# A written order of all engines extended from step 21 to step 95, with a DMA turn from unit 14 on: windowed attention and two expert layers on one core

## The chip, the core and the metric

The kernel runs on one core of a Trainium2 chip. A core has five engines that each run their own instructions in order and meet only through semaphores: TensorE (PE in the profile, with its weight loads as PEld) for matmuls, VectorE (DVE), ScalarE (ACT), GpSimd (POOL) and SyncE (SP), which here issues nearly all DMAs. Matmuls read SBUF and write PSUM; ACT and DVE read PSUM, so everything that PE makes passes through one of them. The metric is the device time of one execution in microseconds (us), lower is better; the profile of one execution tells where it went.

## The reference, cut to what matters

```python
# attention: 4 batches, 8 heads, 576 positions, 64 wide; each row sees itself and the 63 before it
scores = q @ k.T / 8;  scores = where(0 <= i - j < 64, scores, -1e9)
attn = exp(scores - max);  attn = attn / (sum(attn) + 1e-9);  x = attn @ v      # x: 2304 x 512
# first layer, 512 -> 2048 -> 512
h = x @ w_in;  g = h if h >= 1 else 0 if h <= -1 else (h + 1)**2 / 4;  x2 = g @ w_out
# second layer: each row goes to the one of 8 experts with the largest x2 @ w_gate
out[row] = gate_w[row] * (relu(x2[row] @ w1[e]) @ w2[e])
```

All inputs are float32 and the result is float32.

## The kernel before

**Precision.** A float32 factor is kept as two fp32r tiles, hi and lo, and a product is made of three passes (hi·hi, lo weight·hi, hi·lo). So x, the weights and g exist twice, and the lo part is a subtraction on DVE (or POOL).

**Blocks and steps.** The 2304 rows are cut into seven blocks of 256, 384, 256, 256, 384, 384 and 384 rows. A *step* of the first layer handles one of 16 slices of 128 hidden columns for one block: `layer1` (L413, 12 matmuls of 256 or 384 columns into PSUM tile `h`), the gate function on ACT and DVE (L424, L425, L428, L434, L436: `a`, then `ghi` and `glo`), and `layer2` (L455, 6 or 9 matmuls of 512 columns into `acc`). The list `SEG` orders the 112 steps: steps 0 to 5 are block 0's first six slices, 6 to 21 block 1, 22 to 31 the rest of block 0, then 16 steps each for blocks 2 (from step 32), 3 (48), 4 (64), 5 (80) and 6 (96). The second layer has 48 steps of the same shape for the most frequent expert, and a tail for the rows of the others.

**Units.** The x of a block comes from attention *units*: unit 2c + hf is four heads of 128 rows. A unit is `u_qk` (mask and score products L275 and L281, small matmuls, into the one PSUM tile `S`), row maximum (L293, DVE; L304, ACT), exponentials (L314, ACT), reciprocal and normalization (L323, L324 and L327), a turn of the 128x512 attention tile, `av` (L370, small matmuls with v) and the hi and lo parts of x (L382 on ACT, L384 on DVE). All units of a block must be done before the block's first step reads them.

**The turn.** Below `DT0` = 24 the turn is four TensorE transposes into PSUM (L351, tile `pt`) and a copy on ACT (L354, `pb`). From unit 24 on DVE first parts the float32 tile into two planes of 16 bits (`halves`, L172, tile `pp`), SP issues a DMA transpose (L334, `pt<-pp`), and ACT joins the planes (`halves`, L170, `pb`).

**The order.** `HEAD` is a written list of short names (`qk0`, `mx0`, `exp0`, `tr0`, `av0` and so on for units, `ab`, `s`, `hc`, `wl` for splitting a weight tile, `ga`, `rl`, `st`, `gh`, `gl`, `gb` for the parts of a step). It covers units 0 to 9, all 32 weight tiles and steps 0 to 21; `in_order` chains its instructions on PE, DVE, ACT and POOL. From step 22 on a loop writes the steps, `PLAN`, `STAGES` and `STAGES3` say in which half step each part of a unit is written, and the framework's scheduler places the instructions on the engines by its own estimates. Loads of q and k (two buffers) and v (one buffer) are written behind `u_qk` and `u_av` by `run_slot`. `BEHIND` ties the mask products of unit 10 to their written place.

**Other places that the change touches.** Units 5, 7, 9, 10, 11 and 13 are normalized on POOL (`NORM_P`, `NORM_V`), all others on DVE. `evac1` takes a finished block from `acc` to `r` (in the new code `take` does: the first tile on ACT, the second on DVE) and writes it twice to DRAM: whole (`x2s`) and as planes (`x2p`). Tiles 0 and 11 of that are parted on DVE, others on ACT (`PS_V`). The x of every block lies in one of two buffers of the pool `xp` (tag `xT`).

Of the kernel before, what the change touches and what calls it, by code (L numbers as in the profile page):

```python
# [19 lines left out]
P = 128  # L20
# [8 lines left out]
NG = TB * P  # L29
# [7 lines left out]
PLAN = {2: (46, 58), 3: (56, 84), 4: (86, 116), 5: (124, 150), 6: (154, 178)}  # L37
# [4 lines left out]
PS_V = (0, 11, 12, 14, 16)  # L42
PJ_V = (6, 16, 32)
PL_V = ()
DT0 = 24
ST3 = (-1, 0, 1, 2, 6, 7)
US_A = (0, 3, 4, 5, 7, 11, 21)
UJ_V = ()
# [8 lines left out]
BEHIND = 10  # L57
# [21 lines left out]
).split()  # L79
NORM_V = (0, 1, 2, 3, 4, 6, 8, 12, 14, 32)  # L80
NORM_P = 14
# [40 lines left out]
def kernel(  # L122
# [132 lines left out]
    def u_qk(u):  # L255
# [12 lines left out]
        for pr in range(2):  # L268
# [4 lines left out]
            for a, r, rows, o in outs:  # L273
                m = 1 + a if kind == 1 + r else 0
                mm = nc.tensor.matmul(  # L275
                    o, ib[rows, 64 * a:64 * a + 64], mb[rows, m], start=True, stop=False
                )
                if u == BEHIND:
                    tc.keep_in_program_order(mm)
# [27 lines left out]
    u_mask = whole(mask_parts)  # L307

# [11 lines left out]
    def norm_parts(u):  # L320
        s = U[u]
        rc = att.tile([P, 4], F32, tag="rc", name="rc", bufs=2)
        nc.vector.tensor_scalar(out=rc, in0=s["sm"], scalar1=1e-9, scalar2=None, op0=ALU.add)  # L323
        nc.vector.reciprocal(rc, rc)  # L324
        yield
        eng = nc.gpsimd if u < NORM_P and u not in NORM_V else nc.vector
        eng.tensor_tensor(  # L327
            out=s["sr"], in0=s["sr"], in1=rc.unsqueeze(2).to_broadcast([P, 4, P]), op=ALU.mult
        )
        if u >= DT0:  # L330
            pl = att.tile([P, 2, 512], U16, tag="t", name="pp", bufs=2)
# [5 lines left out]
            s["tt"] = tt  # L337

    u_norm = whole(norm_parts)

    def tr_parts(u):
        s = U[u]
        if u >= DT0:
            pb = att.tile([P, 4, P], F32, tag="pb", name="pb")
            halves(nc.vector if u in UJ_V else nc.scalar, s["tt"], pb.rearrange("p h q -> p (h q)"), False)
# [10 lines left out]

    u_tr = whole(tr_parts)

    def av_parts(u):
# [17 lines left out]
        if b not in xT:  # L377
            xT[b] = xp.tile([P, 2, KD, NG], F32R, tag="xT", name="xT")
# [6 lines left out]

    u_av = whole(av_parts)
# [14 lines left out]

    STAGES = [(0, u_qk), (0, u_mask), (1, u_exp), (2, u_norm), (3, u_tr), (4, u_av)]
    STAGES3 = list(zip(ST3, (u_qk, u_mask, u_exp, u_norm, u_tr, u_av)))

# [60 lines left out]
    def evac1(b, acc, partial):  # L465
        t0, n = blocks[b]
        nt = n // P
        for p0 in range(0, nt, 2):
            m = min(2, nt - p0)
            r = part.pop((b, p0), None)  # L470
            add = r is not None
            if r is None:
                r = sp.tile([P, 2, 512], F32, tag="st", name="xrow") if not partial else sp.tile([P, 2, 512], F32, tag="st", name="prow")
            for t in range(m):
                if add:
                    nc.vector.tensor_tensor(out=r[:, t], in0=acc[p0 + t], in1=r[:, t], op=ALU.add)
                elif t == 0:
                    nc.scalar.activation(r[:, t], acc[p0 + t], ACTF.Copy)
                else:
                    nc.vector.tensor_copy(r[:, t], acc[p0 + t])  # L480
            if partial:
                part[b, p0] = r
                continue
            for t in range(m):

                o = t0 + (p0 + t) * P
                xr = x2p[o:o + P].rearrange("p (i h q) -> p i h q", i=2, h=2)
                rr = r[:, t].rearrange("p (i q) -> p i q", i=2)
                if "p2" in Z:
                    for i in range(2):  # L490
                        pl = Z["p2"].tile([P, 2, 256], U16, tag="tt", name="pl", bufs=3)
                        halves(nc.vector if o // P in PS_V else nc.scalar, pl, rr[:, i], True)
                        nc.sync.dma_start(xr[:, i], pl)
                    continue
                pl = att.tile([P, 2, 2, 256], U16, tag="t", name="pl", bufs=2)
                eng = nc.vector if o // P in PS_V else nc.scalar
                xv = rr.bitcast(U16).rearrange("p i (q h) -> p i h q", h=2)
                eng.tensor_copy(pl, xv) if eng is nc.vector else eng.activation(pl, xv, ACTF.Copy)
                nc.sync.dma_start(xr, pl)
            if True:  # L500
# [3 lines left out]
                )  # L504

# [330 lines left out]
    ub_ = {}  # L836
    for u, (b, _, _) in enumerate(units):
        ub_.setdefault(b, []).append(u)
# [13 lines left out]
    def plan(us, s0, s1):  # L852
# [240 lines left out]
```

## Time and profile before

| | |
|---|---|
| median of 3 runs (range) | 734.39 us (734.27 to 735.67) |
| the profiled execution | 735.58 us, span of its instructions 733.8 us |
| busy share of the span: PE, DVE, ACT, POOL | 96%, 60%, 55%, 12% |
| granted TensorE clock, mean | 0.982 |
| DMA | 76.85 MB, mean 105 GB/s |

The page also cuts the span into 40 slices with a busy digit for each engine. PE's digits are 5, 7, 9, 7 in the first four slices and 9 in every later one, so what idles on PE idles in the first 73 us. One caution belongs to the page: matmuls are pipelined and their modelled ends overlap the next start, so a busy PE need not be PE at its peak. A timeline therefore has to be read by starts: from the start of one group of matmuls to the start of the next.

### The profile page before, as it was taken

The page shows a single profiled execution, that of the slowest core. Times are in us where ns is not written, and L with a number is a line of the kernel's source. Part 1 is how long each engine was busy: PE and PEld are TensorE (multiplying, and loading weights), DVE is VectorE, ACT ScalarE, POOL GpSimd, SP SyncE. Part 2 cuts the span into 40 slices and gives each one's busy share as a digit, 9 for nine tenths or more (in the row PEclk, how much of TensorE's full clock was granted, in tenths as well). Part 3 has the DMA queues.
Part 4 walks back from the last instruction along what each step waited for, and adds up shares of the span by engine and source line. Part 5 has one row for each costly group of instructions (what it writes and reads, how often), then busy time and mean ns, then how long its engine had stood idle before and what let it go on. Part 6 is the DMA issues. An engine that isn't in the chain of part 4 may idle for free. (4 is left out here: it accounts for less than half of the span.)

```text
span 733.8 us, 12894 instructions
## 1 busy us (share of the span) xinstructions
PE 705.4 (96%) x4843; PEld 614.0 (84%) x4843; DVE 438.2 (60%) x1028; ACT 405.8 (55%) x1004; POOL 88.5 (12%) x86
## 2 busy tenths in 40 slices
PE   5797999999999999999999999999999999999996
PEld 3676998888888888888888898988888989888985
DVE  6898999345344434552554326988799989551110
ACT  6786776577556656774667445566432515163212
POOL 0021000010000000000000000465130202075000
PEclk9697999999999999999999999999999999999999
DMA  9983102324112312531343403353433324043101
GB/s 334 402 344 116 58 1 59 102 87 155 48 33 71 117 48 51 152 94 44 79 152 69 162 1 122 101 141 90 127 82 94 77 82 102 29 151 115 44 0 55
DMA packets 66691, 76.85 MB, mean 105 GB/s; under 512 B 35671, under 2 KB 41559, under 8 KB 66498
## 3 DMA queue, kind: packets, MB, share of 16 engines
q1 hardware_dynamic: 66466, 75.58, 33.1%
q8 instruction: 38, 0.62, 0.4%
q0 software_dynamic: 160, 0.43, 0.2%
q14 instruction: 27, 0.22, 0.1%
HBM read 53.80 MB, written 14.42 MB: 93 GB/s over the span
## 5 line engine op out<-in xcount | busy, mean ns | idle before, releaser
L413 PE MATMUL h<-xT,wi 128*128 128x384 f32 (+1 forms) x1344 | 231.2, 320 | 2.3 <-DVE a L428 1.9
L413 PEld LDWEIGHTS h<-xT,wi 128*128 128x128 f32 x1344 | 213.5, 192 | 15.2 <-DVE a L428 4.2
L455 PE MATMUL acc<-wo,ghi 128*128 128x512 f32 x576 | 154.9, 397 | 0.0
L455 PEld LDWEIGHTS acc<-wo,ghi 128*128 128x128 f32 x576 | 103.7, 188 | 17.6 <-issue 1.5
L550 DVE CUSTOM_DVE_ANT_0 junk<-xg,wgb 128x512 bf16<-128x512 f32 x144 | 114.2, 793 | 3.2
L413 PE MATMUL h<-xT,we 128*128 128x384 f32 x576 | 110.3, 337 | 1.5 <-DVE glo L445 1.5
L413 PEld LDWEIGHTS h<-xT,we 128*128 128x128 f32 x576 | 102.2, 188 | 6.4 <-DVE glo L445 2.2
L428 DVE SCALAR_TENSOR_TENSOR a<-h,a 128x384 f32<-128x384 f32 (+1 forms) x112 | 55.8, 498 | 83.3 <-ACT a L425 82.9
L424 ACT ACTIVATE a<-h,half 128x384 f32<-128x384 f32 (+1 forms) x112 | 59.6, 534 | 60.8 <-PE h L413 58.8
L455 PE MATMUL acc<-wo,glo 128*128 128x512 f32 x288 | 85.3, 394 | 0.0
L436 DVE TENSOR_TENSOR glo<-a,ghi 128x384 fp32r<-128x384 f32 (+1 forms) x106 | 57.9, 547 | 38.3 <-ACT ghi L434 38.1
L455 PE MATMUL acc<-we,ghi 128*128 128x512 f32 x288 | 78.4, 394 | 0.0
L434 ACT ACTIVATE ghi<-a 128x384 fp32r<-128x384 f32 (+1 forms) x112 | 53.1, 476 | 40.6 <-DVE a L428 38.3
L444 ACT ACTIVATE ghi<-h 128x384 fp32r<-128x384 f32 x48 | 23.1, 482 | 75.9 <-PE h L413 65.2
L455 PEld LDWEIGHTS acc<-wo,glo 128*128 128x128 f32 x288 | 53.7, 188 | 12.1 <-issue 0.2
L624 POOL TENSOR_TENSOR we<-er,we 128x512 fp32r<-128x512 f32 x16 | 23.5, 1472 | 312.9 <-PE h L413 300.7
L455 PEld LDWEIGHTS acc<-we,ghi 128*128 128x128 f32 x288 | 53.1, 188 | 8.1
L445 DVE SCALAR_TENSOR_TENSOR glo<-h,ghi 128x384 fp32r<-128x384 f32 x48 | 26.7, 555 | 53.1 <-ACT ghi L444 53.1
L425 ACT ACTIVATE a<-a 128x384 f32<-128x384 f32 (+1 forms) x112 | 53.5, 479 | 3.0
L314 ACT ACTIVATE sr<-S,nm 128x128 f32<-128x128 f32 x136 | 48.2, 367 | 1.2
L455 PE MATMUL acc<-we,glo 128*128 128x512 f32 x144 | 44.1, 395 | 0.0
L891 POOL TENSOR_TENSOR xT<-xj,xT 128x256 fp32r<-128x256 f32 x36 | 31.2, 875 | 88.3 <-ACT xT L890 88.3
(148 smaller groups left out, 690.1 us busy)
## 6 DMA issues: line engine op xcount, KB each, us to landing
qk<-in_qq_dram SPq DMA_DIRECT2D x26, 320.0 KB, 3.1
er<-in_w_dram SPq DMA_DIRECT2D x32, 256.0 KB, 2.8
wraw<-in_wi_dram SPq DMA_DIRECT2D x14, 512.0 KB, 8.0
wraw<-in_wo_dram SPq DMA_DIRECT2D x14, 512.0 KB, 8.0
vt<-in_vv_dram SPq DMA_DIRECT2D x26, 256.0 KB, 2.7
xg<-x2s SPq DMA_DIRECT2D x18, 256.0 KB, 2.8
out_dram<-y SPq DMA_DIRECT2D x18, 256.0 KB, 2.4
qqr<-in_qq_dram SPq DMA_DIRECT2D x10, 320.0 KB, 7.0
```

Of the source, the lines that this page charges most:

```text
L314: nc.scalar.activation(sr[:, h], s["S"][h % 2][:, h // 2 * P:h // 2 * P + P], ACTF.Exp, scale=0.125, bias=s["nm"][:, h:h + 1], accum_out=s ...
L413: nc.tensor.matmul(h[:, :n], w[:, wa, k * P:k * P + P], x[:, xa, k, :n], start=(i == 0), stop=(i == 3 * KD - 1),)
L424: nc.scalar.activation(a[:, :n], h[:, :n], ACTF.Relu, scale=0.5, bias=half[:, 0:1])
L425: nc.scalar.activation(a[:, :n], a[:, :n], ACTF.Square)
L428: nc.vector.scalar_tensor_tensor(out=a[:, :n], in0=h[:, :n], scalar=1.0, in1=a[:, :n], op0=ALU.max, op1=ALU.min)
L434: nc.scalar.activation(hi[:, :n], a[:, :n], ACTF.Copy)
L436: (nc.gpsimd if pool else nc.vector).tensor_tensor(out=lo[:, :n], in0=a[:, :n], in1=hi[:, :n].bitcast(F32), op=ALU.subtract)
L445: nc.vector.scalar_tensor_tensor(out=lo[:, :n], in0=h[:, :n], scalar=0.0, in1=hi[:, :n].bitcast(F32), op0=ALU.max, op1=ALU.subtract,)
L455: nc.tensor.matmul(a, ga[:, t * P:t * P + P], w[:, wa], start=(first and j == 0), stop=(last and j == 2),)
L550: tc.keep_in_program_order(nc.vector.tensor_tensor_reduce(out=junk, in0=xg[t], in1=Z["wgb"][:, e], scale=1.0, scalar=0.0, op0=ALU.mult, op ...
L624: nc.gpsimd.tensor_tensor(out=w[:, 1], in0=raw, in1=w[:, 0].bitcast(F32), op=ALU.subtract)
L891: (nc.vector if 2 * t + i in PL_V else nc.gpsimd).tensor_tensor(out=lo, in0=r, in1=hi.bitcast(F32), op=ALU.subtract)
```

## The change

`HEAD` is extended from step 21 to step 95 and takes in units 10 to 35, with the loads of q, k (`qq`) and v as names of their own and the evacuation of a block in named parts (`ev`, `evd`, `pl`, `ps`). `PLAN`, the stage lists and `BEHIND` go. `DT0` becomes 14, so units 14 to 23 turn by DMA as units 24 to 35 did, and the parting of the planes, the DMA and the joining are three names (`pp`, `tr`, `pb`). Every normalization is on DVE. Block 2's x gets a buffer of its own, `xq`, in the tag that held the last raw weight tiles. Inside `HEAD` all planes of the evacuation are parted on ACT. Steps 96 on are written by the loop as before.

```diff
-PLAN = {2: (46, 58), 3: (56, 84), 4: (86, 116), 5: (124, 150), 6: (154, 178)}
-DT0 = 24
-ST3 = (-1, 0, 1, 2, 6, 7)
-US_A = (0, 3, 4, 5, 7, 11, 21)
+DT0 = 14
-BEHIND = 10
 HEAD = (
...
+    "gl21 qk10 qq12 ga22 mx10 nm10 exp10 gb20 rl22 rc10 nrm10 st22 qk11 gh22 qq13 ga23 mx11 gl22 "
+    "nm11 exp11 tr10 gb21 pb10 rc11 rl23 nrm11 av10 st23 ev0_21 v11 qk12 gh23 evd0_21 hi10 qq14 "
...
 ).split()
-NORM_V = (0, 1, 2, 3, 4, 6, 8, 12, 14, 32)
-NORM_P = 14
...
-        eng = nc.gpsimd if u < NORM_P and u not in NORM_V else nc.vector
-        eng.tensor_tensor(
+        nc.vector.tensor_tensor(
             out=s["sr"], in0=s["sr"], in1=rc.unsqueeze(2).to_broadcast([P, 4, P]), op=ALU.mult
         )
...
+    def tr_parts(u):
+        s = U[u]
         if u >= DT0:
             pl = att.tile([P, 2, 512], U16, tag="t", name="pp", bufs=2)
-            halves(nc.scalar if u in US_A else nc.vector, pl, s["sr"].rearrange("p h k -> p (h k)"), True)
             tt = att.tile([P, 2, 512], U16, tag="t", name="pt", bufs=2)
+            halves(nc.vector, pl, s.pop("sr").rearrange("p h k -> p (h k)"), True)
+            yield
             nc.sync.dma_start(
                 tt.rearrange("p h (c q) -> p (h c) q", q=P), pl.rearrange("p h q -> p (h q)"), transpose=True
             )
+            yield
             pb = att.tile([P, 4, P], F32, tag="pb", name="pb")
-            halves(nc.vector if u in UJ_V else nc.scalar, s["tt"], pb.rearrange("p h q -> p (h q)"), False)
+            halves(nc.scalar, tt, pb.rearrange("p h q -> p (h q)"), False)
...
-            xT[b] = xp.tile([P, 2, KD, NG], F32R, tag="xT", name="xT")
+            xT[b] = (
+                att.tile([P, 2, KD, 256], F32R, tag="qs", name="xq", bufs=QB)
+                if b == 2
+                else xp.tile([P, 2, KD, NG], F32R, tag="xT", name="xT")
+            )
...
+    def pair_parts(b, p0, acc):
+        t0, n = blocks[b]
+        m = len(acc)
+        r = part.pop((b, p0), None)
+        if r is not None:
+            for t in range(m):
+                nc.vector.tensor_tensor(out=r[:, t], in0=acc[t], in1=r[:, t], op=ALU.add)
+        else:
+            r = sp.tile([P, 2, 512], F32, tag="st", name="xrow")
+            take(r, 0, acc[0])
+            if m == 2:
+                yield
+                take(r, 1, acc[1])
+        yield r
+        for t in range(m):
+            pl = att.tile([P, 2, 2, 256], U16, tag="t", name="pl", bufs=2)
+            nc.scalar.activation(pl, xv, ACTF.Copy)
+            yield
+            nc.sync.dma_start(xr, pl)
...
+        if name in ("qq", "v"):
+            (u_load if name == "qq" else v_load)(k)
+            continue
```

What stands on the engines is shown at three places, before first and then now, without the leading numbers.

PE, around unit 17's score product, before: steps 36 and 37. `S<-qk` are its score matmuls, `h` and `acc` the matmuls of the two layers, `av` unit 15's value product, `pt<-ct,sr` unit 16's turn by TensorE.

```order
L281 MATMUL S<-qk 64x128 x3
L413 MATMUL h<-xT,wi 128x256 x8
L370 MATMUL av<-pb,vt 64x64 x8
L413 MATMUL h<-xT,wi 128x256 x4
L455 MATMUL acc<-wo,ghi 128x512 x4
L455 MATMUL acc<-wo,glo 128x512 x2
L413 MATMUL h<-xT,wi 128x256 x12
L455 MATMUL acc<-wo,ghi 128x512 x3
L351 MATMUL pt<-ct,sr 128x128 x4
```

PE, around unit 16's score product and unit 15's value product, now: up to step 39.

```order
L320 MATMUL S<-qk 64x128 x4
L489 MATMUL acc<-wo,ghi 128x512 x4
L489 MATMUL acc<-wo,glo 128x512 x2
L404 MATMUL av<-pb,vt 64x64 x8
L447 MATMUL h<-xq,wi 128x256 x12
```

Before, three of a product's score matmuls stand apart from the other five (which follow three steps later), a value product stands inside a `layer1`, and a turn inside a `layer2`; now each product stands whole, between whole groups of the layers, and this unit's turn is no longer on PE.

ACT, around the joining or copying of unit 14's turned tile `pb`, before. `a` and `ghi` belong to steps, `nm`, `sr` and `xT` to units, `pl` to the evacuation of block 0.

```order
L382 ACTIVATE xT<-av 128x2x128
L304 ACTIVATE nm<-mx 128x4
L314 ACTIVATE sr,sm<-S,nm 128x128 x4
L498 ACTIVATE pl<-prow 128x1024
L354 ACTIVATE pb<-pt 128x512
L424 ACTIVATE a<-h,half 128x256 x2
```

ACT, around unit 14's `pb`, now.

```order
L468 ACTIVATE ghi<-a 128x256 x2
L458 ACTIVATE a<-h,half 128x256
L459 ACTIVATE a<-a 128x256
L211 ACTIVATE pb<-pt 128x2x512
L468 ACTIVATE ghi<-a 128x256
```

The copy out of PSUM has become a joining of planes that waits for a DMA, and a step's `ghi` stands behind it.

DVE, units 7 to 9 in the first 60 us, before. `rc` is unit 7's reciprocal, `mx` unit 8's maximum, `a` and `t` belong to a step and a weight tile.

```order
L323 TENSOR_SCALAR rc<-sm 128x4
L324 RECIPROCAL rc<-rc 128x4
L428 SCALAR_TENSOR_TENSOR a<-h,a 128x256
L293 TENSOR_REDUCE mx<-S 128x2x2
L203 TENSOR_SCALAR t<-t 128x512
```

The same place now.

```order
L360 TENSOR_SCALAR rc<-sm 128x4
L361 RECIPROCAL rc<-rc 128x4
L462 SCALAR_TENSOR_TENSOR a<-h,a 128x256
L363 TENSOR_TENSOR sr<-sr,rc 128x512
L332 TENSOR_REDUCE mx<-S 128x2x2
```

Unit 7's normalization `sr<-sr,rc`, which was on POOL, stands ahead of unit 8's maximum; units 5 and 9 get theirs in the same way.

## Rows read from the trace of the kernel before

**Rows 1.** Busy time by stage (stretch, its length, engines, granted clock, DMA):

```profile
0.00:121.50 121.50, 102.69 (x828) 87.43 (x829) 107.34 (x206) 88.88 (x231) 8.46 (x13) 0.90 0.54 198
121.50:437.00 315.50, 315.32 (x2573) 271.06 (x2572) 141.10 (x321) 194.48 (x535) 3.13 (x3) 1.00 0.29 85
```

**Rows 2.** What PE waited for, 0 to 80 and 80 to 460 us:

```profile
PE pt L351 <- DVE xT L384: 5.9, 4, 2.7
...
PE h L413 <- DVE a L428: 0.2, 1, 0.2
```

**Rows 3.** Timeline of PE, a turn alone: start, length, matmuls, count

```profile
152.54 1.09 PE L455 MATMUL acc<-wo,ghi 128*128 128x512 f32 x4
153.46 0.60 PE L351 MATMUL pt<-ct,sr 128*128 128x128 f32 x4
153.82 0.71 PE L455 MATMUL acc<-wo,glo 128*128 128x512 f32 x2
154.37 1.60 PE L413 MATMUL h<-xT,wi 128*128 128x256 f32 x12
155.80 0.86 PE L455 MATMUL acc<-wo,ghi 128*128 128x512 f32 x3
```

**Rows 4.** Timeline of PE, a whole score product:

```profile
285.57 0.62 PE L455 MATMUL acc<-wo,glo 128*128 128x512 f32 x2
...
286.80 1.48 PE L413 MATMUL h<-xT,wi 128*128 128x384 f32 x7
```

**Rows 5.** Timeline of PE, unit 17's score product in two pieces:

```profile
185.29 0.62 PE L455 MATMUL acc<-wo,glo 128*128 128x512 f32 x2
...
186.24 1.22 PE L413 MATMUL h<-xT,wi 128*128 128x256 f32 x8
...
197.31 1.12 PE L413 MATMUL h<-xT,wi 128*128 128x256 f32 x8
198.36 0.32 PE L281 MATMUL S<-qk 64*64 64x128 f32 x1
...
199.00 1.20 PE L455 MATMUL acc<-wo,ghi 128*128 128x512 f32 x4
```

**Rows 6.** Timeline of PE, a score product cut by a turn:

```profile
217.25 1.36 PE L413 MATMUL h<-xT,wi 128*128 128x256 f32 x10
...
218.93 0.66 PE L351 MATMUL pt<-ct,sr 128*128 128x128 f32 x4
...
220.16 1.20 PE L455 MATMUL acc<-wo,ghi 128*128 128x512 f32 x4
```

**Rows 7.** The parts of a turn on ACT and DVE: count, ns min/median/max, first to last

```profile
L354 ACT ACTIVATE pb<-pt x24: 576/597/667, 10.5 to 267.2; 128x512 f32<-128x512 f32 x24
L170 ACT ACTIVATE pb<-pt x12: 1351/1370/1394, 288.3 to 404.5; 128x1024 uint16<-128x1024 uint16 x12
L172 DVE COPY pp<-sr x12: 682/685/696, 284.4 to 400.7; 128x1024 uint16<-128x1024 uint16 x12
```

**Rows 8.** The DMA turn's line L334: issues, who waited, landing

```profile
L334 SPq DMA_TRANSPOSE pt<-pp x12: 1232/1233/1338, 285.1 to 401.4; - x12
  ACT pb L170: 8.6, 7
DMA to landing us min/median/max: 3.0/3.1/4.8
```

**Rows 9.** Timeline of POOL and DVE in the first 60 us:

```profile
28.60 0.69 DVE L206 SCALAR_TENSOR_TENSOR t<-wraw,t 128x512 int32<-128x512 int32 x1
30.49 1.03 POOL L327 TENSOR_TENSOR sr<-sr,rc 128x512 f32<-128x512 f32 x1 [30.03 <-DVE rc L324]
30.66 1.42 DVE L206 SCALAR_TENSOR_TENSOR t<-wraw,t 128x512 int32<-128x512 int32 x1
41.86 0.68 DVE L327 TENSOR_TENSOR sr<-sr,rc 128x512 f32<-128x512 f32 x1
58.51 0.64 DVE L203 TENSOR_SCALAR t<-t 128x512 int32<-128x512 int32 x1 [0.92 <-ACT t L201]
```

More of the change, by code (lines that the diff above doesn't have):

```diff
@@ L274, in u_qk @@
                 m = 1 + a if kind == 1 + r else 0
-                mm = nc.tensor.matmul(
+                nc.tensor.matmul(
                     o, ib[rows, 64 * a:64 * a + 64], mb[rows, m], start=True, stop=False
                 )
-                if u == BEHIND:
-                    tc.keep_in_program_order(mm)
             for a, r, rows, o in outs:
@@ L336, in norm_parts @@
             )
[L337 to L343, printed above, removed]
+            del pl
+            yield
             pb = att.tile([P, 4, P], F32, tag="pb", name="pb")
-            halves(nc.vector if u in UJ_V else nc.scalar, s["tt"], pb.rearrange("p h q -> p (h q)"), False)
+            halves(nc.scalar, tt, pb.rearrange("p h q -> p (h q)"), False)
             s["pb"] = pb
@@ L355, in tr_parts @@
         s["pb"] = pb
-    u_tr = whole(tr_parts)
     def av_parts(u):
@@ L463, with take @@
     part = {}
-    def evac1(b, acc, partial):
-        t0, n = blocks[b]
[L467 to L473, printed above, removed]
-            for t in range(m):
[L475 to L483, printed above, removed]
+    def take(r, t, a):
+        if t == 0:
+            nc.scalar.activation(r[:, t], a, ACTF.Copy)
+        else:
+            nc.vector.tensor_copy(r[:, t], a)
@@ L484, in evac1 @@
+    def evac1(b, acc):
+        t0, n = blocks[b]
+        for p0 in range(0, n // P, 2):
+            m = min(2, n // P - p0)
+            r = sp.tile([P, 2, 512], F32, tag="st", name="xrow")
+            for t in range(m):
+                take(r, t, acc[p0 + t])
             for t in range(m):
@@ L488, in evac1 @@
                 rr = r[:, t].rearrange("p (i q) -> p i q", i=2)
[L489 to L500, printed above, removed]
-                o = t0 + p0 * P
-                nc.sync.dma_start(
-                    x2s[o:o + m * P].rearrange("(a p) d -> p a d", p=P), r[:, :m]
-                )
+                for i in range(2):
+                    pl = Z["p2"].tile([P, 2, 256], U16, tag="tt", name="pl", bufs=3)
+                    halves(nc.vector if o // P in PS_V else nc.scalar, pl, rr[:, i], True)
+                    nc.sync.dma_start(xr[:, i], pl)
+            o = t0 + p0 * P
+            nc.sync.dma_start(
+                x2s[o:o + m * P].rearrange("(a p) d -> p a d", p=P), r[:, :m]
+            )
     Z = {}
@@ L835 @@
             (v_load if x[0] == "v" else u_load)(int(x[1:]))
-    ub_ = {}
-    for u, (b, _, _) in enumerate(units):
-        ub_.setdefault(b, []).append(u)
     steps, seg0 = [], {}
@@ L850 @@
     slots = {}
-    def plan(us, s0, s1):
-        for i, u in enumerate(us):
-            st = s0 + ((s1 - 6 - s0) * i) // max(1, len(us) - 1)
-            for off, fn in STAGES if u < DT0 else STAGES3:
-                slots.setdefault(st + off, []).append((fn, (u,)))
     def at(s, fn, *a):
         slots.setdefault(s, []).append((fn, a))
-    for b in range(1, NB):
-        if b in PLAN:
-            plan(ub_[b], base + PLAN[b][0], base + PLAN[b][1])
-            continue
-        s0 = base + 2 * seg0[b - 1]
-        plan(ub_[b], s0, s0 + 32)
     W2 = {}
@@ L942, in run_slot @@
             fn(*a)
-            if fn is u_qk and a[0] + RB >= EARLY:
-                u_load(a[0] + RB)
-            if fn is u_av and a[0] + VB >= EARLY:
-                v_load(a[0] + VB)
     def in_order(traced):
@@ L968, in evac @@
     def evac(i):
-        ph, b, _, _, last, partial = steps[i]
+        ph, b, _, _, last, _ = steps[i]
         if last and ph == 1:
-            evac1(b, acc.pop((ph, b)), partial)
+            evac1(b, acc.pop((ph, b)))
         elif last:
@@ L975, in step_parts @@
     def step_parts(i):
-        _, b, f = steps[i][:3]
+        _, b, f, _, last, partial = steps[i]
         n = blocks[b][1]
         g[i] = yield from act_parts(xT[b], win[f], n, i in GLO_P)
+        if f == KF - 1:
+            del xT[b]
         yield
         second(i)
+        if last:
+            a = acc.pop((1, b))
+            for p0 in range(0, len(a), 2):
+                key = i, p0
+                left[key] = pair_parts(b, p0, a[p0:p0 + 2])
+                if partial:
+                    kept[i] = b, p0
+            del a
         yield
-        evac(i)
-        yield
-    head = {}
+    head, left, kept = {}, {}, {}
     bb = nc.cur_bb.bb
@@ L990 @@
         k = int(x[len(name):])
-        key = "w" if name in ("ab", "s", "hc", "wl") else "g" if name[0] == "g" or name in ("rl", "st", "ev") else "u", k
+        if name in ("qq", "v"):
+            (u_load if name == "qq" else v_load)(k)
+            continue
+        if name[-1] == "_":
+            t = int(name.strip("evdpls_"))
+            gen = left[k, t - t % 2]
+            r = next(gen, None)
+            if r is not None and k in kept:
+                part[kept.pop(k)] = r
+                del left[k, t - t % 2]
+            del gen, r
+            continue
+        key = "w" if name in ("ab", "s", "hc", "wl") else "g" if name[0] == "g" or name in ("rl", "st") else "u", k
         if key not in head:
```

24 lines of the change are left out of this document (14 added, 10 removed), and 80 rows, old and new, of the table HEAD.

## The prediction

> **What bounds the kernel now.** I read the busy time by stage first. From 121.5 us (the end of step 21's first layer) to 437.0 us (the start of step 96) PE is busy for 315.32 of 315.50 us, while ACT is busy for 194.48 and DVE for 141.10 [rows 1]. The list of waits agrees: from 80 to 460 us PE waits 0.2 us for another engine, once [rows 2]. So in the stretch that the change rewrites, the end moves only if PE's own work gets shorter, and nothing on ACT, DVE or the queues counts until it makes PE wait. In the first 121.5 us it is otherwise: PE is busy for 102.69 us, DVE for 107.34, and PE's largest wait there is for DVE (5.9 us before four turns) [rows 1, 2].
>
> Busy does not mean useful. I therefore read the timeline of PE by starts. In undisturbed groups an `acc` matmul takes 0.23 us (four from 152.54 to 153.46) and an `h` matmul of 256 columns 0.119 (twelve from 154.37 to 155.80) [rows 3]. Whatever stands between such groups is priced by the start of what follows it.
>
> **A turn on PE.** The four transposes run from 153.46 to 153.82, 0.36 us, and the two `acc` matmuls behind them take 0.55 instead of 0.46, so 0.09 is lost on the way back: 0.45 us for one turn [rows 3]. The change takes ten of them (units 14 to 23) off PE: 10 x 0.45 = 4.5 us. The listed length of those four transposes is 0.60 us, because each runs under the next; it is not what they cost.
>
> The Trainium skill has a price that speaks for more. Its page "TensorE: Matmul & The Clock Gate" (Part 4: PE-mode transpose) gives some 275 ns for one such transpose. By that, 40 of them would be an estimated 11.0 us and the whole time about 720. Four in 0.36 us are 0.09 each here, so the row decides.
>
> **Whole products instead of pieces.** A whole score product (masks and scores of a unit) takes from 286.03 (two `acc` matmuls after 285.57) to 286.80, 0.77 us [rows 4]. Unit 17's lies in two pieces: from 185.75 to 186.24, and from 198.26 (eight `h` matmuls after 197.31) to 199.00, together 1.23, so the cut costs 0.46, and 0.1 more for one more way back [rows 5]. One that a turn cuts lasts from 218.44 to 220.16, 1.72 us, where 0.77 + 0.36 would do: 0.59 [rows 3, 4, 6]. Counted in the instruction order from step 21 on, 12 of the 26 units from 10 to 35 are cut before, and none after. Five are cut by matmuls of the layers; measured like unit 17's they cost 0.2 to 0.5 us each, 1.9 together, and 0.5 for the five extra ways back. Three are cut by a turn, 1.6 together. Four are cut by a value product, 0.1 to 0.35 each, 1.0 together. Sum 5.0 us. Bounds: 4.0 if the four cuts by a value product give nothing, 7.1 if all twelve cost what the dearest does. How many products stand next to a value product hardly changes (10 before, 10 after), so no more is counted there. PE's own work in this stretch thus falls by 9.5 us. All other matmuls stay, and from step 96 on PE's order is the same up to one exchange of two groups in the last pass.
>
> **What DMA turns add elsewhere.** For ten units DVE gets a parting of 0.69 us, ACT's copy of 0.60 becomes a joining of 1.37, and SP gets an issue of 1.23 with the data there 3.1 us after it [rows 7, 8]. That is 6.9 us on DVE and 7.7 on ACT, in a stretch where they have 174 and 121 us to spare [rows 1], so by amount it costs nothing. The danger is place: on ACT the joining waits for the DMA, and behind it stand a step's `a` and `ghi`, for which PE's `acc` matmuls wait. From the start of the parting to landing it is 0.69 + 3.1 = 3.8 us. In the written order about one and a half steps stand between parting and joining (unit 14: from before `st31` to behind `rl33`). A step of a 256-row block is 12 x 0.12 + 6 x 0.23 = 2.8 us [rows 3], so the data is there by then, or some tenths late. `ga` runs two steps ahead of `gb`, so ACT has about two steps, 5.6 us, for its 1.3 us of a step's work and whatever stands in between. In the trace ACT waits 8.6 us for 7 of 12 turns, and PE waits 0.2 us in all [rows 2, 8]: cover of this kind does hold.
>
> **Other edits.** The loads now stand in the written order of SP. Behind a v load that waits for the single buffer stand the next turn and the next q; the written order gives it a step or more of time, as before. Block 2's own x buffer lets its units write x while block 0 is still read; PE did not wait there before [rows 2], so nothing is gained. Planes of two tiles parted on ACT instead of DVE: nothing, ACT has room. The large load of the gate's weights stands on SP behind the last turn in both orders; it starts when the last unit is done, which is now later by the order, with the steps in between for cover. For all of this and the DMA turns I add 0.8 us of new waits on PE: ACT's 8.6 us over 12 turns are 0.72 each, 7.2 for ten, and I let about a tenth through. Bounds: 0, since all of it may be covered, and the 14.9 of the second rival.
>
> **Normalization in the head.** Units 5, 7 and 9 move from POOL to DVE, 0.68 us each [rows 9], in the stretch where PE waits for DVE. For unit 5 it is free: while POOL ran it (30.49 to 31.52), a DVE operation that began at 30.66 took 1.42 instead of 0.69 as at 28.60, and that 0.73 comes back. The other two delay DVE by 1.4 us, of which the pause of 0.92 before 58.51 takes up some [rows 9]. I take +0.5; bounds -0.7 (only the return counts) and +2.0 (all three, no return). On this the Trainium skill's page "SBUF — State Buffer" (SBUF: two separate sides) says that a POOL operation and a DVE operation with two SBUF inputs exclude each other for a whole instruction. The collision agrees with that; if the others collided too, the head would gain about 0.2 instead of losing 0.5.
>
> **Sum.** Against the profiled execution, 735.6 us (span 733.8 and 1.8 around it): 735.6 - 4.5 - 5.0 + 0.5 + 0.8 = 727.4. That execution lies 1.2 above the median of 734.4, so the forecast is 726.2 us as a median.
>
> **Rivals.**
> 1. *Half is given back.* The scheduler placed instructions by its estimates and left PE 0.2 us of waits; a written order cannot be better informed at each of 74 steps, and where it holds PE for an `acc` buffer or for `glo` it stalls. Or the cuts filled time in which PE would have waited anyway, so that only the turns count: 735.6 - 4.5 + 0.5 + 0.8 - 1.2 = 731.2. For it: the pieces look like what a scheduler does with work that is ready. Against it: pieces cost time between starts without any listed wait.
> 2. *Slower by the joining on ACT.* If the wait for the DMA and the longer joining reach PE at each of the ten units, that is 10 x (0.72 + 0.77) = 14.9 us, and the time 726.2 - 0.8 + 14.9 = 740.3. It turns the sign once all 26 units cost PE more than 9.0/26 = 0.35 us each. For it: steps of 256 rows are shorter than those of 384 in which the turn has run so far, and ACT is the busier of the two helpers. Against it: 121 us of room on ACT and two steps of lead.
> 3. *Nothing measurable.* New waits of 8 to 10 us eat the gain; 734.4.
> 4. *More than forecast.* The head gains (-0.7) and no wait is added: 735.6 - 9.5 - 0.7 - 1.2 = 724.2. With all cuts at the dearest price 722.1.
> The change might also not do what it says; the instruction order shows the turns gone from PE and the pieces joined, so that has no chance of its own.
>
> **How the numbers follow.** Forecast (about 724.5 to 729) 0.55, half given back (729 to 732.9) 0.20, nothing 0.09, slower 0.12, more than forecast 0.04 (the skill's transpose price within it, 0.01). A measurement of this kernel tells some 0.2%, 1.5 us, from no change. Faster: 0.55 + 0.20 + 0.04 = 0.79; same 0.09; slower 0.12. The range from 722.5 to 733.0 takes in the bounds of the first term and the half-given-back case and leaves out the cases of nothing and of slower, 0.21.
>
> **What would show it.** Steps 22 to 95 should take some 307 us instead of 315.5, with 16 PE transposes left in them (units 10 to 13), whole groups of score matmuls, and PE's waits there under 2 us. ACT's wait for `pt<-pp` should be under 1 us a turn. The head should end within 1 us of before, and from step 96 on nothing should move. I am wrong if PE's list of waits shows `glo` or `acc` buffers for several us between 121 and 437, or if the stretch loses its cuts and does not get shorter.

## The result, and the profile after

The changed kernel takes 728.05 us (median of 5 runs, 726.16 to 730.36) against 734.39 before; the ratio is 0.991 (95% interval 0.989 to 0.994), 6.3 us less. It is faster by 0.9%, which the interval sets clear of no change; the forecast was 726.2, so 1.9 us of the gain are missing, and the time lies inside the range. The profiled execution takes 728.3 us with a span of 726.5, 7.3 less than the span before.

By stages (busy time of the engines, columns as in [rows 1]) the changed kernel has its step 21 at 120.42 us and its step 96 at 426.76:

```profile
0.00:120.42 120.42, 104.32 (x828) 88.93 (x829) 107.34 (x209) 89.09 (x231) 5.48 (x10) 0.90 0.54 200
120.42:426.76 306.34, 306.34 (x2533) 265.45 (x2532) 145.99 (x325) 203.18 (x537) 0.00 (x0) 1.00 0.34 95
426.76:726.50 299.74, 288.17 (x1444) 255.15 (x1442) 191.18 (x508) 122.13 (x239) 76.98 (x70) 0.99 0.30 88
```

and before, the last stage alone (the others are in [rows 1]):

```profile
437.00:733.80 296.80, 287.39 (x1444) 255.48 (x1442) 189.73 (x502) 122.48 (x239) 76.92 (x70) 1.00 0.30 87
```

The head (up to the start of step 21) is 1.1 us shorter, the stretch from step 21 to step 96 is 9.1 shorter (315.48 to 306.34), and the tail behind it 3.0 longer (296.8 to 299.7), with the same 1444 matmuls. The longer tail was not in the forecast. In the stretch PE is busy all the time; from 80 to 426 us no wait of PE is listed at all. The DMA turns show there as a wait of ACT alone (waits: total, times, longest; then the issue of the turns and their landing), to be read beside [rows 8]:

```profile
ACT pb L211 <- DMA pt<-pp: 5.6, 8, 1.0
```

```profile
L375 SPq DMA_TRANSPOSE pt<-pp x22: 1233/1239/2060, 170.4 to 413.7; - x22
...
DMA to landing us min/median/max: 3.0/3.1/4.0
```

What PE waits for in the tail, after and then before:

```profile
PE h L447 <- DVE glo L479: 3.1, 4, 1.5
PE h L447 <- DVE a L462: 2.4, 4, 0.9
```

```profile
PE h L413 <- DVE a L428: 1.7, 3, 0.7
PE h L413 <- DVE glo L445: 1.5, 2, 1.3
```

The waits grow by 2.3 us, all of them for DVE, which there computes the gate (the choice of the expert) beside its part of each step.

### The profile page after: what moved, and what is told of

Same layout as the page of the kernel before. It is cut to its first block, busy times and chain, and to the rows that moved or that the text cites. A ratio compares the mean times of both kernels' runs of the same rounds, so it can differ in the third digit from the quotient of the medians.

```text
span 726.5 us, 12818 instructions
## 1 busy us (share of the span) xinstructions
PE 698.8 (96%) x4803; PEld 609.5 (84%) x4803; DVE 444.5 (61%) x1042; ACT 414.4 (57%) x1006; POOL 82.5 (11%) x80
## 5 line engine op out<-in xcount | busy, mean ns | idle before, releaser
L447 PE MATMUL h<-xT,wi 128*128 128x384 f32 (+1 forms) x1152 | 202.6, 326 | 2.5 <-DVE a L462 2.4
L447 PEld LDWEIGHTS h<-xT,wi 128*128 128x128 f32 x1152 | 188.7, 193 | 13.1 <-DVE a L462 4.7
L605 DVE CUSTOM_DVE_ANT_0 junk<-xg,wgb 128x512 bf16<-128x512 f32 x144 | 112.2, 779 | 3.6 <-DMA xg<-x2s 0.4
L332 DVE TENSOR_REDUCE mx<-S 128x4 f32<-128x512 f32 x34 | 23.4, 689 | 31.0 <-PE S L320 31.0
```

What stands on the lines that cost most here:

```text
L332: nc.vector.tensor_reduce(out=mx.rearrange("p (b a) -> p a b", a=2), in_=s["S2"][:, :, :2 * P].rearrange("p a (b k) -> p a b k", b=2), axi ...
L447: nc.tensor.matmul(h[:, :n], w[:, wa, k * P:k * P + P], x[:, xa, k, :n], start=(i == 0), stop=(i == 3 * KD - 1),)
L605: tc.keep_in_program_order(nc.vector.tensor_tensor_reduce(out=junk, in0=xg[t], in1=Z["wgb"][:, e], scale=1.0, scalar=0.0, op0=ALU.mult, op ...
```

## The experiments

The table has for each kernel the median, its ratio to the kernel before and, from starts of the layer matmuls on PE, the lengths of steps 0 to 13, of steps 21 to 95 and of the tail. The last three columns are explained under the tail: where the packet of PE code nearest to the end of block 6 falls (us behind the start of step 112, the first of the second layer), after how long the last `x2s` write there lands (from its issue until all of it is there), and how long steps 120 to 123 take. The lengths are those of one profiled execution each and the medians those of 3 to 12 runs, so the two need not move alike (cut_late: 732.81 profiled, 734.72 the median). A *piece* below is whatever PE does between two layer matmuls, priced from where the next layer matmul could have started.

| kernel | median us | ratio (95%) | 0 to 13 | 21 to 95 | 96 to end | packet | landing | 120 to 123 |
|---|---|---|---|---|---|---|---|---|
| before | 734.39 | 1 | 66.24 | 315.49 | 296.78 | 6.25 | 3.06 | 18.17 |
| after | 728.05 | 0.991 (0.989 to 0.994) | 66.08 | 306.34 | 299.77 | 16.54 | 4.99 | 19.90 |
| turns_on_pe | 729.42 | 0.993 (0.992 to 0.995) | 66.03 | 310.55 | 297.14 | 6.22 | 3.03 | 18.35 |
| cut_products | 732.01 | 0.998 (0.997 to 0.999) | 65.97 | 311.95 | 298.43 | 16.52 | 4.99 | 20.02 |
| cut_late | 734.72 | 1.001 (0.999 to 1.002) | 66.78 | 312.67 | 298.47 | 16.54 | 4.99 | 19.91 |
| free_order | 741.02 | 1.009 (1.007 to 1.012) | 70.57 | 314.36 | 299.08 | 15.81 | 4.71 | 19.98 |
| before_dt14 | 734.78 | 1.000 (0.999 to 1.002) | 66.26 | 312.67 | 299.61 | 16.00 | 4.92 | 20.03 |
| early_join | 762.40 | 1.039 (1.038 to 1.041) | 66.09 | 340.03 | 301.06 | 16.50 | 4.98 | 23.03 |
| all_turns | 734.72 | 1.001 (1.000 to 1.002) | 65.54 | 314.45 | 299.28 | 18.60 | 3.06 | 19.91 |
| old_start | 727.25 | 0.991 (0.989 to 0.992) | 66.21 | 306.33 | 298.57 | 16.55 | 4.99 | 19.91 |
| norms_pool | 728.54 | 0.993 (0.992 to 0.994) | 66.09 | 306.33 | 300.27 | 16.03 | 4.90 | 19.96 |
| more_pe_code | 725.72 | 0.989 (0.987 to 0.990) | 66.35 | 307.26 | 296.31 | 8.22 | 3.24 | 18.17 |
| more_pe_32 | 724.98 | 0.987 (0.986 to 0.989) | 66.59 | 306.34 | 297.48 | 8.48 | 3.14 | 18.15 |
| before_more_pe | 736.14 | 1.003 (1.002 to 1.004) | 66.93 | 315.87 | 296.95 | 17.46 | 3.05 | 18.57 |

### The turns

`turns_on_pe`: `DT0` back to 24, the ten `pp` names gone, each `tr` one group of matmuls ahead of its `pb`.

```diff
-DT0 = 14
+DT0 = 24
-... nrm14 ga32 pp14 tr14 st31 gb30 rl32 gh31 st32 gl31 ga33 gh32 gl32 gb31 rl33 pb14 ...
+... nrm14 ga32 st31 gb30 rl32 gh31 st32 gl31 ga33 gh32 gl32 tr14 gb31 rl33 pb14 ...
```

> The changed kernel with one part undone: the turns of units 14 to 23 go back from the DMA to PE (four transposes each, placed one group of matmuls ahead of ACT's copy); order, cuts and head stay as in the changed kernel. Theory: a turn on PE costs 0.45 us between starts (0.36 for four transposes, 0.09 on the way back), so PE's excursions between step 21 and step 96 grow by 4.5 us and the time goes from 728.0 to about 732.5. Rival one: what a turn frees on PE is taken back by waits elsewhere, and the time stays within 1.5 us of 728.0. Rival two, by the price of 275 ns for a PE-mode transpose in the Trainium skill's page 'TensorE: Matmul & The Clock Gate' (Part 4): 11.0 us more, 739.

The stretch grew by 4.21 us, 0.42 a turn, so the term stands. A turn alone reads as it did before [rows 3]: 0.35 to the next start, and four `acc` matmuls of 1.01 instead of 0.92 behind it (timeline of PE).

```profile
206.80 0.60 PE L386 MATMUL pt<-ct,sr 128*128 128x128 f32 x4
207.15 1.17 PE L488 MATMUL acc<-wo,ghi 128*128 128x512 f32 x4
208.16 0.62 PE L488 MATMUL acc<-wo,glo 128*128 128x512 f32 x2
```

The 11.0 us that one would estimate from the some 275 ns of the Trainium skill's page "TensorE: Matmul & The Clock Gate" (Part 4: PE-mode transpose; measured there on a 128x128 bf16 tile) are not there. But the span rose by 2.4 only, and the median by 1.4, since the tail became 2.6 shorter, and no turn of these lies in the tail.

`before_dt14`: the kernel before with `DT0 = 14` and nothing else.

> The kernel before the change with one part of it done alone: turns by DMA from unit 14 instead of 24; order by the scheduler and its planned stages as before. Theory: the ten turns are worth 0.42 each here as well, so PE's excursions from step 21 to 96 fall by some 4.2 us, as far as the scheduler cuts no more products than before, and the time is 730 to 731. Rival: the stages planned for DMA turns give less time in blocks of 256 rows than in those of 384; where the joining comes too early on ACT, PE waits as in early_join (half of ACT's wait for the DMA reaches PE there), and the gain of 4.2 is eaten: 733 or more.

The stretch fell by 2.8 of the 4.2, and the tail grew by 2.8, so nothing is left. The 1.4 that the stretch did not give are about PE's one wait there, and ACT waits 16.8 us for the DMA where the changed kernel's ACT waits 5.6:

```profile
PE h L413 <- DVE a L428: 1.5, 1, 1.5
...
ACT pb L170 <- DMA pt<-pp: 16.8, 13, 3.7
```

### The order

`free_order`: `in_order` chains only what is named ahead of `qk10`.

```diff
+    if x == "qk10": fixed = {i.name for i in bb.instructions}
...
-    i for i in bb.instructions if i.name not in seen
+    i for i in bb.instructions if i.name in fixed and i.name not in seen
```

> The changed kernel with the written order binding on PE, ACT, DVE and POOL only up to step 21; behind it the instructions are handed over in the same order, but the scheduler may place them by its estimates, as before the change. SP's order, the DMA turns from unit 14 and the third block's buffer stay. Theory: the scheduler cuts products again and the time rises by up to the 5.0 us of the cuts, to 731 to 733; the stretch from step 21 to step 96 then takes 309 to 311 us instead of 306.3. Rival: the order itself is worth nothing, the time stays within 1.5 us of 728.0 with as many whole products, and what the stretch gained beyond the turns came with the handing over in another order. If it runs faster than 726.5, the written order costs waits that the scheduler avoids.

The written order is worth more than expected: 8.0 us in the stretch. Between layer matmuls PE has 61 pieces of 44.7 us in the place of 46 of 38.9, so 5.8 of it are pieces. The head lost 4.5 as well: work of later units is now placed in it (between the starts of steps 0 and 14 PE runs 148 matmuls into `S` in the place of 96, and is busy for 61.3 us in the place of 56.9). The stretch is thus slower with less to do.

`cut_products` puts a `yield` between the two halves of `u_qk` and names the first half ahead of the group of layer matmuls before it; `cut_late` puts the `yield` behind the second four masks.

```diff
-    def u_qk(u):
+    def qk_parts(u):
...
+            if pr == 0 and u in CUT: yield
...
-"... ga34 gl33 ... qk15 ..."
+"... qa15 ga34 gl33 ... qk15 ..."
```

> The changed kernel with one part undone and more than undone: 21 of the 22 score products of units 14 to 35 are cut in two, by moving each product's first half (its first four masks and four scores) ahead of the group of layer matmuls (one: of a value product) that stands before it. Work and all other orders are the same. Theory: a cut makes the product dear by itself, 0.2 to 0.5 us, and brings one more way back of 0.1: at the mean of the five measured ones (0.48) 21 x 0.48 = 10.1 us more, 738; at unit 17's 0.56, 11.8 more, 740. Rival: a cut costs only the second way back, 21 x 0.1 = 2.1 us, 730, and most of the 5.0 us that the prediction gave to whole products came from elsewhere.

> The kernel of cut_products with the same 21 cuts four scores later in time: behind the second four masks instead of ahead of them, so that the pieces are 16 and 8 records of PE instead of 12 and 12. In cut_products a cut costs 0.21 us in PE's excursions (0.49 + 0.49 against 0.77) and 5.6 us in the stretch. Theory: a cut's price hangs on its place; unit 17 before the change was cut here and took 0.73 + 0.48, 0.44 more than a whole one, so 21 x 0.44 = 9.3 in the excursions and 9 to 11 in the stretch, 735 to 739. Rival: every cut costs the same 0.2, the stretch grows by 5 to 6 and the time stays near 732.

The first costs 5.6 us in the stretch for 21 cuts, 0.27 each; the second 6.3, 0.30 each. Both miss the expected 10 and both are over 2.1. In cut_products a half of 12 records stands alone (timeline of PE as in [rows 3]):

```profile
199.15 0.62 PE L492 MATMUL acc<-wo,glo 128*128 128x512 f32 x2
199.69 0.25 PE L317 MATMUL S<-cb 64*64 64x128 bf16 x4
199.77 0.39 PE L321 MATMUL S<-qk 64*64 64x128 f32 x8
200.09 1.70 PE L450 MATMUL h<-xq,wi 128*128 128x256 f32 x12
```

From 199.61 (two `acc` of 0.23 behind 199.15) to 200.09 it takes 0.48, two of them 0.96 against 0.77 for a whole one. The expectation of cut_late was built on a misreading. Before, unit 17 was not cut behind masks but inside a run of scores. Its first piece, in the gap of [rows 5], was four masks and six of eight score records:

```profile
185.84 0.25 PE L275 MATMUL S<-cb 64*64 64x128 bf16 x4
185.92 0.39 PE L281 MATMUL S<-qk 64*64 64x128 f32 x6
```

With the rest that is 0.49 + 0.74. My cuts lie where masks and scores change anyway and are the cheap kind; the scheduler's lay anywhere. No run cuts at such a place by design, but the pieces in the traces show that the number of records does not set the price: 16 records take 0.73 in the kernel before, where the scheduler left two pieces of 2 scores, 2 masks, 6 scores, 2 masks and 4 scores, and 0.55 in cut_late (4 masks, 8 scores, 4 masks). What sets it stays open.

### The cover of the DMA

`early_join`: `pb` of units 14 to 35 directly behind `tr` (or `av` of the unit before).

```diff
-... pp20 gl47 tr20 ga49 st48 gh48 gl48 gb47 rl49 st49 ga50 gh49 pb20 ...
+... pp20 gl47 tr20 pb20 ga49 st48 gh48 gl48 gb47 rl49 st49 ga50 gh49 ...
```

> The changed kernel with the joining of units 14 to 35 moved ahead in ACT's order, to directly behind the DMA's issue (or behind the value product before, where that frees its buffer), so that ACT waits out nearly the whole DMA each time. It measures the cover that the prediction reckoned with. Theory (two steps of lead, and 99 us of room on ACT from step 21 to step 96): ACT's wait for the DMA grows from 5.6 us over 8 turns to 40 to 65 us over 22, some 2 to 3 each, and PE waits less than 3 us for it in all. Rival (the second one of the prediction: what stands behind the joining reaches PE): each us of wait on ACT beyond about 1 is paid by PE, 22 x 1 to 2, 20 to 45 us more.

ACT's wait grew by 69 us, and the stretch by 33.7, half of that. PE stands idle for 25.8 of them (busy for 314.2 of 340.0 us):

```profile
ACT pb L210 <- DMA pt<-pp: 74.8, 21, 4.9
...
PE acc L488 <- ACT ghi L467: 12.8, 8, 4.0
PE S L315 <- ACT sr L350: 4.3, 3, 3.3
```

The other 7.9 are PE itself: it is busy for 314.2 us in the place of 306.3. Three times in this stretch, for 3.4 us each (from 176.3, 299.2 and 381.1), its granted clock is about 0.50, the lower of its two levels (1.2 of 2.4 GHz), each time soon after a wait of PE (2.3, 4.0 and 3.6 us); half of these 10.2 us, an estimate, is 5.1 of the 7.9.

So the 103 us in which the changed kernel's ACT is idle in the stretch are no cover for a wait in the middle of its queue, and the second rival's mechanism is real. The changed kernel escapes it by place alone. In its trace a value product starts 0.3 to 8.1 us behind the end of its joining, in the median of the 22 units 1.7: that is its margin, not two steps.

`all_turns`: `DT0 = 10`, `pp` and `tr` of units 10 to 13 behind `nrm`.

```diff
-DT0 = 14
+DT0 = 10
-... rc10 nrm10 st22 qk11 gh22 qq13 ga23 mx11 gl22 nm11 exp11 tr10 gb21 pb10 ...
+... rc10 nrm10 pp10 tr10 st22 qk11 gh22 qq13 ga23 mx11 gl22 nm11 exp11 gb21 pb10 ...
```

> The changed kernel with four more turns, those of units 10 to 13, taken off PE and put on the DMA, with parting and issue directly behind the unit's normalization and the joining where it was. Theory: 0.42 to 0.45 us each as measured for the ten others, 1.7 to 1.8 us less between step 21 and step 96, as these steps have the same room on ACT and DVE; the end follows unless the tail shifts. Rival: the steps from 22 to 31 of the first block leave less time between issue and joining (unit 10: one score product, one first and one second layer, some 3.6 us, against 0.69 + 3.1 needed), so that PE waits for what stands behind the joining on ACT, by up to 0.5 us per unit; no gain.

The stretch is 8.1 us longer, all of it before step 31. ACT's and PE's waits up to 175 us have the larger part:

```profile
ACT pl L527 <- DMA pt<-pp: 4.6, 2, 2.5
...
PE av L403 <- ACT nm L342: 4.1, 1, 4.1
PE av L403 <- ACT pb L210: 3.2, 3, 1.2
```

Block 1's evacuation takes its planes `pl` from the two buffers of tag `t` that `pp` and `pt` of a turn use; on ACT it waits for the turn's data, and with it the next unit behind it. That sharing is the cause is argued from these lines; a third buffer was not tried. PE's waits are 7.3 us. In the first it stands idle from 145.5 to 149.6, and from 147.7 to 154.5 its granted clock is 0.50, the lower level. There a value product, six `acc` and twelve `h` matmuls take 5.8 us from start to start (from 149.60), where the changed kernel takes 3.6 for the same (from 153.05). The four turns give back an estimated 1.7, at 0.42 each. Together that is 7.8 of the 8.1.

### The head

`norms_pool` puts three normalizations back on POOL; `old_start` puts the first 64 names of `HEAD` back.

```diff
-        nc.vector.tensor_tensor(
+        (nc.gpsimd if u in (5, 7, 9) else nc.vector).tensor_tensor(
```

```diff
-"... exp0 nm1 qk2 rc0 exp1 nrm0 tr0 ab0 qk3 mx2 rc1 ..."
+"... exp0 nm1 rc0 qk2 exp1 nrm0 mx2 tr0 ab0 qk3 rc1 ..."
```

> The changed kernel with the normalization of units 5, 7 and 9 put back on POOL, as before the change; the order is the changed kernel's. The start of step 0 moves by up to 1 us with the first loads from run to run, so the time from step 0 to step 14 is what counts: 66.08 us in the changed kernel, 66.24 before the change. Theory of the prediction: the norms cost DVE 0.5 us there, so this kernel takes 65.6. Rival one: nothing hangs on them, 66.0 to 66.2. Rival two: POOL's operation blocks DVE beside it and the three cost more there, 66.5 to 67.5.

> The changed kernel with the written order of its first 64 pieces (up to the first layer of step 0) as it was before the change: among them the row maximum of unit 2 ahead of unit 0's turn and ab0, and unit 3's transposes behind ab2. Everything from step 0 on is the changed kernel's. The trace of the changed kernel has step 0 at 25.04 us and before the change at 25.97, which the prediction did not reckon with. Theory: it is this order, so step 0 comes 0.9 us later, and as PE hardly waits from there on for DVE work that catches up, 0.5 to 0.9 of it reach step 21 and the end: 728.5 to 729.0. Rival one: step 0 stays at 25.0, and the 0.9 was a difference of one execution. Rival two: step 0 is 0.9 later, but step 21 is not, because DVE is what bounds the head in between.

Neither matters: steps 0 to 13 take 66.09 and 66.21 against 66.08. The start of step 0 lies anywhere from 23.8 to 26.0 us in the fourteen traces, and from 23.8 to 25.9 in kernels whose first instructions are alike. The changed kernel's 0.9 there lies within this spread, whose cause was not looked into.

### The tail

DVE's waits in the tail hold a line that grows by 1.8 us, near the 1.7 by which steps 120 to 123 grow: a wait for a plane buffer, which is free when the write before it has landed. After and before:

```profile
DVE pl L213 <- DMA x2p<-pl: 4.4, 1, 4.4
```

```profile
DVE pl L172 <- DMA x2p<-pl: 2.6, 1, 2.6
```

The DMA view of the 8 us around these writes has a strip of GB/s and the queues. After, from 510.66 us:

```profile
GB/s 0 0 0 41 10 346 367 387 367 387 418 347 357 428 336 337 326 423 326 316 296 36 10 10 5 20 25 25 20 25 0 0 0 0 0 82 336 235 112 346
...
q8 instruction: 1, 0.02, 0.7%
...
x2s<-xrow SPq DMA_DIRECT2D x1, 256.0 KB, 5.0
```

Before, from 519.95 us:

```profile
GB/s 0 0 0 0 0 356 366 366 417 356 417 377 346 417 366 316 356 341 331 336 336 61 0 0 0 0 36 321 280 199 321 153 295 326 41 20 5 4 67 151
...
x2s<-xrow SPq DMA_DIRECT2D x1, 256.0 KB, 3.1
```

Before, 16 DMA engines write at some 360 GB/s and stop together. After, a packet of 16 KB on the instruction queue q8 comes in between (of another such queue, q14, either view has one small packet), and behind the full rate stand eight slices of 0.2 us at 5 to 25, about what one engine of the 16 moves: as the strip reads, one finishes its share alone, 1.9 us late. In the kernel before, that packet falls ten us earlier, when neither write has begun. From the 4.4 us on DVE runs late: the `glo` that ends 20.1 us behind the start of step 112 in the kernel before ends at 21.8 now, DVE has the same pauses from there to step 120 in either trace (2.3 us), and in steps 120 to 123 PE waits 1.7 us for DVE's `glo`, against 0.3 before. There are 38 such packets in either kernel, one for some 256 matmuls and weight loads of PE, so I read them as PE's code; the change moves them because it takes instructions off PE. The next two kernels are made to move them and nothing else: idle matmuls ahead of the warming ones, 40 in `more_pe_code`, 32 in `more_pe_32`; `before_more_pe` has 76 in the kernel before.

```diff
+    for i in range(40):
+        nc.tensor.matmul(wzp[:, :8], wz[:, :P], wz[:, :8], start=True, stop=True)
     for i in range(WARM):
```

> The changed kernel with 40 idle matmuls of 8 columns on PE ahead of its ten warming ones, while PE waits for the first load anyway; nothing reads them. It moves the places at which PE's instructions are fetched (packets of 16 KB on the instruction queue q8, one every 256 PE instructions) by some two steps. In the traces of the changed kernel, of old_start and of cut_products such a packet falls 16.5 us behind the start of step 112, into the write of block 6's rows; the write of x2s lands after 5.0 us instead of 3.0 and DVE waits 4.4 us for a plane buffer. In the trace of before and in turns_on_pe the packet falls at 6.2 us, the write lands after 3.0, DVE waits 2.7, and steps 120 to 123 are 1.7 us shorter. Theory: it is this fetch; with the packet moved away the wait is 2.7 again, the stretch from step 96 to the end loses 1.7 to 2.1 us of its 299.8, and the median goes from 728.0 to about 726. Rival: the tail's loss comes from the phase between PE and the gate's work on DVE, with the fetch a bystander; then the tail stays at 298.5 to 299.8 and the time within 1 us of 728.0.

The packet moved to 8.2 us, the write lands after 3.2, steps 120 to 123 take 18.17, the tail 296.3 and the median is 725.72. With 40, however, another packet met the turn of unit 20 (DMA view from 226.6 us, and PE's wait):

```profile
q8 instruction: 1, 0.02, 1.2%
...
pt<-pp SPq DMA_TRANSPOSE x1, 4.4
```

```profile
PE av L404 <- ACT pb L211: 0.6, 1, 0.6
```

> The changed kernel with 32 idle matmuls of 8 columns ahead of the warming ones instead of the 40 of more_pe_code, nothing else. With 40, the fetches of PE's code miss the write behind step 112 and the tail takes 296.3 us, but one falls 2.0 us into the DMA turn of unit 20, which lands after 4.45 us instead of 3.07, and PE waits 0.8 for its value product. Theory: with 32 every fetch comes 16 instructions later, so that this one falls near or behind the landing (3.1 us or more), while the one at step 112 stays ahead of the writes (some 9.8 us behind the step's start; they begin at 13.1). The stretch from step 21 to 96 then takes 306.3 to 306.6 again and the tail 296 to 297: a median of 724.5 to 725.3. Rival: the 0.8 has nothing to do with the fetch and stays, 725.7.

The stretch is 306.34 again and the median 724.98 (724.36 to 725.78): faster than the kernel before, and by its runs than the changed kernel, whose fastest is 726.16. The two were not run side by side, and the intervals of their ratios to the kernel before just overlap (0.986 to 0.989 and 0.989 to 0.994). Its DVE wait is back as well:

```profile
DVE pl L213 <- DMA x2p<-pl: 2.6, 1, 2.6
```

Of the 2.9 us by which its span is shorter than the changed kernel's, the tail is 2.3; step 0 also starts 1.2 earlier, within its spread, and steps 0 to 13 take 0.5 longer. Its tail is still 1.2 longer than that of more_pe_code, all of it in steps 144 to 147 (19.04 against 17.85; 17.84 to 17.92 in the other traces). There a packet falls 1.8 us behind the start of step 144, and ACT waits up to 4.1 us for a load of weights in the place of 2.7 in the changed kernel. How many idle matmuls are best is therefore a matter of where all 38 packets fall.

> The kernel before the change with 76 idle matmuls of 8 columns ahead of the warming ones, all orders otherwise the same. They move PE's code fetches by 152 instructions, so that one should fall some 16 us behind the start of step 112, where it falls in the changed kernel; in the kernel before it falls at 6.2. Theory (the fetch, and not the change's order, is what costs the changed kernel 1.7 us behind step 119): DVE's wait for a plane buffer behind step 112 grows from 2.6 to 4.4 us, steps 120 to 123 take 1.7 us longer, the tail 298.4 to 299.5 instead of 296.8, and the median rises by 1.5 to 2, to about 736. Rival: the kernel before is not open to this, since its gate's work stands in another order; no change of more than 0.5 in the tail.

`before_more_pe` missed its aim. The packet fell at 17.46, behind the landing of the `x2s` write and ahead of the next three plane writes (from 17.5), and the tail stayed at 296.95. The median rose by 1.9 all the same; the profile has 1.0 of it, 0.7 in steps 0 to 13, and its cause is open. What it was to show, `before_dt14` shows beside its turns: the gate in the order of before, the packet at 16.00, steps 120 to 123 in 20.03. Over all fourteen kernels, those with the packet from 15.8 to 16.6 or at 18.6 take 19.9 or more there, the five others 18.15 to 18.57. At 18.6 (all_turns) the packet falls on the last plane writes, which land after 3.1 to 3.6 us in the place of 1.7, while DVE's wait for a plane buffer is the short one, 2.6; DVE then waits 3.5 us for ACT's `gex`, where it waits 1.7 before and after. The 23.03 of early_join has 3.4 us at the lower granted clock in it.

## Why the prediction was right, point by point

- *Turns, -4.5.* Right, 4.2 (turns_on_pe).
- *Whole products, -5.0.* Right: 9.15 less the 4.21 of the turns leaves 4.9, and nearly all of it is PE's own work. What stands between layer matmuls falls from 56 pieces of 47.3 us to 46 of 38.9, 8.4 in all; with the turns on PE in both (turns_on_pe: 54 of 42.6) it still falls by 4.7. By the pieces in the trace of the kernel before, set against whole ones of now, the five products cut by layers cost 1.9 (as forecast, with 0.5 more for the ways back), the three cut by a turn 1.6, the four cut by a value product 1.0; 0.3 more lies in whole products next to a value product. The price of a single clean cut is 0.27 to 0.30 instead of the 0.42 assumed on average, so the scheduler's cuts were dearer than clean ones.
- *New waits on PE, +0.8.* None came in the stretch. The reason given (two steps of lead, room on ACT) was wrong though the number was near: early_join shows that the stretch pays for half of a wait on ACT, and the changed kernel's own trace that the margin is 1.7 us a turn.
- *Normalizations, +0.5.* Failed, 0.0 (norms_pool). The start's spread of 2 us is larger than the term and was not in the sum.
- *From step 96 on nothing moves.* Failed, and this is most of the miss: +3.0. The order of PE there was indeed the same; what moved is the place of its code fetches. Of the 3.0, steps 120 to 123 are 1.7 and steps 116 to 119 0.5 (17.21 against 16.75), which go with the packet in every trace. The rest are steps 104 to 107 (18.64 against 17.71), and they go with another packet. It falls 3.1 to 4.1 us ahead of step 104 in four kernels (after, before_dt14, free_order, norms_pool), which take 18.13 to 18.64 there; the ten others have none in that place and take 16.95 to 17.71, of them more_pe_code and more_pe_32 17.41 and 17.40. In the four, ACT's longest wait there for a load of an expert's weights is 2.5 to 2.6 us, in the ten 1.3 to 2.0. That the packet acts through this load is argued.
- *Rivals.* The first (a written order cannot be better informed) is refuted by free_order, its other form (only the turns count) by the 4.9. The second did not occur; its mechanism exists. Of the fourth, the added waits stayed away, but the head gained 0.2 and not 0.7.
- *A reading.* 121.5 us is where step 21's first layer starts (121.52), not where it ends; no term hangs on it.

The sum by measured terms on the span: 733.8 - 0.9 (start) - 0.2 (head) - 4.2 - 4.9 + 3.0 = 726.6, as against 726.5. That the forecast came so near is in part luck: the 3.0 of the tail was mostly offset by the 0.9 of the earlier start and by the 1.3 of waits and normalizations that did not come.

## What to carry to other kernels

Read a saving on the bounding engine from starts, and prove it in its own stretch: the end-to-end time carried 1.4 of the 4.2 us of ten turns, because the rest of the program answered by where code fetches fell. When a change adds or removes instructions on one engine, look at the instruction queue's packets around writes whose buffer somebody waits for; a few idle instructions at the start can move them away. A DMA joined in the middle of a busy queue is covered only by what stands between its joining and its first reader, not by that engine's idle share.

## What the runs showed of the hardware

- A 16 KB packet on PE's instruction queue (0.7% of 16 engines over 8 us, so some 0.9 us on one of them) beside a 256 KB write puts the write's landing from 3.1 to 5.0 us, and beside a DMA turn from 3.07 to 4.45 us. The strip behind the full rate fits one of 16 engines being late and the landing waiting for the last. With 32 or 40 idle matmuls that move the packets the tail is 2.3 or 3.5 us shorter (297.48 and 296.31 against 299.77), and the medians are 724.98 and 725.72 against 728.05.
- A piece of a score product does not cost by its length: between layer matmuls 8 records of scores take 0.47 us, 12 of masks and scores 0.49, 16 take 0.55 (or 0.73, by their sequence) and all 24 take 0.77. In free_order 2 records of scores alone still take 0.45, while 2 to 4 records of masks alone take 0.27. So for scores, nearly half a microsecond goes with the coming and going.
